# Loads to both halves of the partitions split in two, and the transposed solutions of both batches in one bank

## The chip, the cores and the metric

The kernel runs on one core of one Trainium2 chip. The metric is the device time of one execution, in microseconds (us). Before the change it was 1447.63 us, the median of three runs (1440.06 to 1449.23).

## The reference

Three stages are chained. The first is a recurrence over 768 time steps on a 40 by 40 state, for 4 batches and 8 heads; the other two are two-layer networks over the 3072 tokens that it yields (320 to 2048 to 320), the first with x·relu6(x+3)/6 between its layers, the second with x·sigmoid(x).

```python
B, H, S, D = 4, 8, 768, 40
for t in range(S):
    kt, vt, rt = (k[:, :, t], v[:, :, t], r[:, :, t])
    wt, at, bt = (w[:, :, t], a[:, :, t], b[:, :, t])
    y[:, :, t] = np.einsum('bhd,bhde->bhe', rt, state)
    Sa = np.einsum('bhde,bhe->bhd', state, at)
    state_decay = state * wt[:, :, None, :] - np.einsum('bhd,bhe->bhde', Sa, bt)
    state = state_decay + np.einsum('bhd,bhe->bhde', vt, kt)
...
h = x @ w_in
g = h * np.clip(h + 3.0, 0.0, 6.0) / 6.0
x = g @ w_out
...
h = x @ w_in
g = h * (1.0 / (1.0 + np.exp(-h)))
return g @ w_out
```

## The kernel before, in words

**The recurrence** is worked in chunks of 32 time steps. A pair of batches is taken at a time; a window is 128 time steps of a pair (12 windows in all), and a chunk, called a step below, is a quarter of a window (48 steps). The steps form a chain, because each starts from the state that the step before left. For each window three things are prepared: products of the decays (`prepare`), the 32 by 32 triangular matrices of all chunks and heads (`windows`, L452), and the inverses of these matrices. For the inverses the matrices go to DRAM (`scr_l`, L476), come back into the tile u with one matrix to a partition (`factors`, L489), are inverted on VectorE in 30 rounds of two operations (`inverses`, L515 and L519), and go back by way of `scr_t` (L535, L540). There are 64 matrices in a window, and each is laid on two partitions, 64 apart, since VectorE inverts one half of the rows on each. So one load of `factors` reads 64 rows of 4 KB twice: its source is broadcast with a leading dimension of two. The tile u has two places; one of them lies in the stage buffer of the weights.

One step of the chain (`steps`), for both batches: L613 makes the right-hand sides, which ScalarE copies to rx; L626 transposes the state; L642 makes the transposed solution and L644 the plain one, batch by batch, into one bank of PSUM for each batch; VectorE copies the transposed solution out (L650, `turned`), ScalarE the plain one (L655, `evac`); L667 needs the transposed solutions of both batches; VectorE masks its result (L675); L692 makes the outputs and the new state from it and from the plain solutions; and the new state is copied out for the next step. The chain has three banks of PSUM.

**The two networks** run in tiles of 256 tokens, 12 tiles for each. In a tile the first product (`first`, L937) has 128 matmuls and the second (`second`, L981) 96. A tile of the first network needs the outputs of one window; the second network starts when the first has ended. The weights come as 64-bit floats, in 16 chunks for each network, and are turned into pairs of 32-bit values by a sequence on VectorE, ScalarE and GpSimd (`convert`, `split`; L780 to L805). A chunk is loaded by three DMAs: L742 and L752 with full width, and L745, which brings rows 256 to 319 of the first matrix to both halves of the partitions, with a source that is broadcast in the same way as that of L489. The first 64 of the last 128 rows are so held twice, for two products at once. The same is done for the last 64 of the 320 channels of the decays (L879) and outputs (L884) in `inputs1`. The weights of the second network lie where the recurrence had its tiles, and are loaded when it has ended.

**The order of the work** is written out before the program is built: the class `Order` keeps a time for each engine, generators ask for an engine with a duration and conditions, and the earliest candidate is taken, by priority. Each engine, and SP, which issues all the DMAs, then works its list in order. The durations of these lists are the planner's; in an engine's list, whatever stands behind an instruction that waits, waits too.

Of the kernel before, what the change touches and what calls it, by code (L numbers as in the profile page):

```python
# [16 lines left out]
B, H, S, D = 4, 8, 768, 40  # L17
BH = B * H
NB = 2
NP = B // NB  # L20
G = NB * H
HP = H // 2
NW, WT, CT = 6, 128, 32
NC = WT // CT
# [7 lines left out]
DM, DFF = H * D, 2048  # L32
NM = DFF // 128
MT = NB * WT
SEG = WT + 1
NWX = 5 * SEG
E0 = 64
# [208 lines left out]
class Kernel:  # L246
# [232 lines left out]
    def factors(self):  # L479

        nc, o = self.nc, self.o
        for n in range(NN):
            k = n % 2 if n > 1 else 0
            u = self.u[k]
            free = [("uo", n - 1) if n < 3 else ("iv", n - 2)] if n else []
            if k:
                free += self.converted
            el = yield ("sp", 524e3, ("lo", n), *free)
            nc.sync.dma_start(out=u.rearrange("p j i -> p (j i)"),  # L489
                              in_=self.scr_l[n % 2].unsqueeze(0).to_broadcast([2, G * NC, CT * CT]))  # L490
            o.ev[("u", n)] = o.t["sp"]
            o.ev[("ul", n)] = el

# [75 lines left out]
    def steps(self, bs, chunks):  # L569

        nc, o = self.nc, self.o
        rxs = [self.rx[32:64, b] for b in range(NB)]
# [9 lines left out]
        def every(conds):  # L582

            return [(b, tuple(c for x in bs for c in conds(x)) if b == bs[0] else ()) for b in bs]
# [4 lines left out]
        for g in chunks:  # L589
            n, c = divmod(g, NC)  # L590
            ga, ysl = self.ga[n % 3], self.ysl[g % 2]
# [7 lines left out]
            if first:  # L599
                for b in bs:  # L600
                    e = yield ("pool", 500.0, *st[b])
# [6 lines left out]
            for b, conds in every(lambda x: (("ga", n), ("v", g), *st[x])):  # L608
                e = yield ("pe", 600.0, "bank", *conds)
                p = o.take()  # L610
                pv = p[:, 0:DM].rearrange("p (h e) -> p h e", h=H)
                for h in range(H):
                    nc.tensor.matmul(out=pv[32:64, h], lhsT=ga[0:KP, b * H + h, c * CT:(c + 1) * CT],  # L613
                                     rhs=self.rhs[0:KP, b, h], start=True, stop=True)
                o.ev[("x0", g, b)] = e

                def evac(p=p, pv=pv, b=b):
                    nc.scalar.activation(out=rxs[b][:, :, 0:D], in_=pv[32:64], func=AF.Copy)
                    o.give(p, o.t["act"] + 190)
                o.one("act", 440.0, [e], evac, ("rx", g, b))  # L620
            for b, conds in [] if first else every(lambda x: st[x]):
                e = yield ("pe", 300.0, "bank", *conds)
                p = o.take()
                pv = p[0:D, 0:DM].rearrange("p (h e) -> p h e", h=H)
# [6 lines left out]
                o.one("act", 440.0, [e], evac, ("st", g, b))  # L631


            for b, conds in every(lambda x: [("rx", g, x)]):
                e = yield ("pe", 1050.0, "bank", *conds)
                p = o.take()
                pv = p[:, 0:DM].rearrange("p (h e) -> p h e", h=H)
                pt = p[:, DM:DM + HP * CT].rearrange("p (h t) -> p h t", h=HP)
                gs = [ga[32:64, b * H + h, c * CT:(c + 1) * CT] for h in range(H)]
                for h in range(H):  # L640
                    r0 = E0 * (h % 2)
                    nc.tensor.matmul(out=pt[r0:r0 + 64, h // 2], lhsT=rxs[b][:, h], rhs=gs[h], start=True, stop=True)  # L642
                for h in range(H):
                    nc.tensor.matmul(out=pv[32:64, h], lhsT=gs[h], rhs=rxs[b][:, h, 0:D], start=True, stop=True)  # L644
                if c == NC - 1:
                    o.ev[("gafree", n, b)] = e
                done = o.share(p, 2)

                def turned(pt=pt, b=b, done=done):
                    nc.vector.tensor_copy(out=self.vr[:, b, 3], in_=pt)  # L650
                    done(o.t["dve"] + 160)
                o.one("dve", 290.0, [e], turned, ("xt", g, b))

                def evac(pv=pv, b=b, done=done):
                    nc.scalar.activation(out=self.ysr[32:64, b, :, CT:RW], in_=pv[32:64], func=AF.Copy, scale=-1.0)  # L655
                    done(o.t["act"] + 190)
                o.one("act", 440.0, [e], evac, ("xv", g, b))


            e = yield ("pe", 40.0 + 215.0 * len(bs), "bank", *[("xt", g, b) for b in bs], ("vr", g, 0), ("vr", g, 1))  # L660
            p = o.take()
            pv = p[:, 0:H * CT].rearrange("p (h t) -> p h t", h=H)
            for h in range(HP):
                for x in range(2):
                    for b in bs:
                        r0 = 64 * b + 32 * x
                        nc.tensor.matmul(out=pv[r0:r0 + 32, 2 * h:2 * h + 2], lhsT=self.vr[0:KP, b, 1 + 2 * x, h],  # L667
                                         rhs=self.vr[0:KP, b, 0::2, h], start=True, stop=True)
            done = o.share(p, len(bs))
# [13 lines left out]
            for b, conds in every(lambda x: (  # L683
# [3 lines left out]
                e = yield ("pe", 600.0, "bank", *conds)  # L687
                p = o.take()
                pv = p[:, 0:4 * RW].rearrange("p (h n) -> p h n", h=4)
                for h in range(4):  # L690
                    for u in range(2):
                        nc.tensor.matmul(out=pv[E0 * u:E0 * u + D, h], lhsT=ysl[0:KP, b, 4 * u + h],  # L692
                                         rhs=self.ysr[0:KP, b, 4 * u + h], start=True, stop=True)
                o.ev[("yse", g, b)] = e
                done = o.share(p, 2)
# [33 lines left out]
    def raws(self, wi, wo, key):  # L729

        nc, cv = self.nc, self.cv
        for m in range(NM):
            if wi.dtype == mybir.dt.float32:
                k, wiv, wov = 1, wi, wo
            else:
                k, wiv, wov = 2, wi.bitcast(I32), wo.bitcast(I32)
            cs = slice(m * 128 * k, (m + 1) * 128 * k)
            raw, free = self.slot("raw0", key, m)
            raw = raw.bitcast(wiv.dtype)
            yield ("sp", 131e3 * k, free and ("cv", key, free[0], 0), ("u", 0) if key == 1 and m >= GR else None,  # L740
                   ("uo", NN - 1) if key == 2 else None)
            nc.sync.dma_start(out=raw[:, 0:256 * k].rearrange("p (j f) -> p j f", j=2),  # L742
                              in_=wiv[0:256, cs].rearrange("(j p) f -> p j f", p=128))
            e = yield ("sp", 66e3 * k)
            nc.sync.dma_start(  # L745
                out=raw[:, 256 * k:384 * k],
                in_=wiv[256:320, cs].unsqueeze(0).to_broadcast([2, 64, 128 * k]))
            self.o.ev[("raw", key, m, 0)] = e
            raw, free = self.slot("raw1", key, m)
            raw = raw.bitcast(wiv.dtype)  # L750
            e = yield ("sp", 164e3 * k, free and ("cv", key, free[0], 1))
            nc.sync.dma_start(out=raw[:, 0:DM * k], in_=wov[m * 128:(m + 1) * 128])  # L752
            self.o.ev[("raw", key, m, 1)] = e
# [111 lines left out]
    def inputs1(self):  # L865

        nc, o = self.nc, self.o
        xs = self.xw[0].rearrange("p (j b t) -> p j b t", j=3, b=NB)
        ws = self.xw[1].rearrange("p (j b t) -> p j b t", j=3, b=NB)
        xf, wf = (x.rearrange("p (j n) -> p j n", j=3) for x in self.xw)  # L870
        for n in range(NN):
            free = ("xp", n - 1) if n else ("cv", 1, K0 - 1, 1)
            sw, sy = self.scr_w[n], self.scr_y[n]
            for b in range(NB):
                r = sw[b * DM:(b + 1) * DM, 0:WT]
                yield ("sp", 131e3, ("wo", n), free, ("cv", 1, K0 - 1, 0))
                nc.sync.dma_start(out=ws[:, 0:2, b], in_=r[0:256].rearrange("(j p) t -> p j t", p=128))
                yield ("sp", 66e3)
                nc.sync.dma_start(out=ws[:, 2, b], in_=r[256:DM].unsqueeze(0).to_broadcast([2, 64, WT]))  # L879
            g = n * NC + NC - 1  # L880
            e1 = yield ("sp", 262e3, *[("yo", g - q, b) for b in range(NB) for q in (0, 2)])
            nc.sync.dma_start(out=xf[:, 0:2], in_=sy[0:256].rearrange("(j p) b t -> p j (b t)", p=128))
            e = yield ("sp", 131e3)
            nc.sync.dma_start(out=xf[:, 2],  # L884
                              in_=sy[256:DM].rearrange("p b t -> p (b t)").unsqueeze(0).to_broadcast([2, 64, MT]))
            xh, xl = self.xh[n % 2], self.xl[n % 2]
            e = yield ("pool", 1840.0, e, e1)
            nc.gpsimd.tensor_tensor(out=xf, in0=xf, in1=wf, op=ALU.mult)
            e = yield ("act", 850.0, e, ("g1", n - 2) if n > 1 else None)
            nc.scalar.activation(out=xh, in_=xf, func=AF.Copy)  # L890
            yield ("pool", 1310.0, e)
            nc.gpsimd.tensor_tensor(out=xl, in0=xf[:, 0:2], in1=xh[:, 0:2].bitcast(F32), op=ALU.subtract)
            e = yield ("pool", 790.0)
            nc.gpsimd.tensor_tensor(out=xh[64:128, 2], in0=xf[64:128, 2], in1=xh[64:128, 2].bitcast(F32),
                                    op=ALU.subtract)
            o.ev[("xp", n)] = o.ev[("x", n)] = e
# [316 lines left out]
```

## Time and profile before

| | |
|---|---|
| median of three runs | 1447.63 us |
| profiled execution, its own time | 1440.64 us |
| span of its trace | 1438.8 us |
| TensorE (PE) busy | 1230.8 us, 86% of the span |
| VectorE (DVE) busy | 792.4 us, 55% |
| ScalarE (ACT) busy | 571.9 us, 40% |
| GpSimd (POOL) busy | 427.8 us, 30% |
| DMA: moved, mean rate | 149.47 MB, 104 GB/s |
| mean granted clock of TensorE | 0.892 |

The profile is of one execution. A busy share is an average over very different stages: in the first stage the weights of the first network are converted and the first windows are prepared; then the recurrence and the first network share TensorE; then the recurrence has ended, the first network is finished and the weights of the second are loaded; at last the second network runs alone. A granted clock of 1.00 is 2.4 GHz and 0.50 is 1.2 GHz, the two levels that TensorE has; a value between them is a mean over time. SPq is the queue of DMA issues: a row of SPq tells how long an issue took, not how long the transfer did; a DMA row of the chain of waits runs from the issue to the landing.

### The profile page before, as it was taken

Reading aid. Unit: us, or ns where it says so; the run is one execution under the profiler, and the core shown is the slowest. Engines: PE = TensorE matmul, PEld = TensorE weight load, DVE = VectorE, ACT = ScalarE, POOL = GpSimd, SP = SyncE. Lnnn points to the kernel's source line nnn. Section 1 sums busy time; section 2 is a strip of 40 time slices with the busy share of each in tenths; the row PEclk is TensorE's granted clock in tenths of the full one; section 3 lists DMA queues with packets and bytes.
Section 4 is the critical chain, followed back from the end, with each engine's and each line's share of the span. In section 5 each row is a group of like instructions: output and inputs, shape, how many; then the busy total and the mean of one; then the engine's idle time right before and its main releaser. Section 6 shows DMA issues by size and latency. Waiting matters only on the chain.

```text
span 1438.8 us, 35403 instructions
## 1 busy us (share of the span) xinstructions
PE 1230.8 (86%) x14582; PEld 1146.6 (80%) x14582; DVE 792.4 (55%) x1852; ACT 571.9 (40%) x1177; POOL 427.8 (30%) x532
## 2 busy tenths in 40 slices
PE   1035658899989998899989999877899999999998
PEld 1034557788878888788878888777799999999998
DVE  6486668585588576686866522377762222222221
ACT  3232334444334333434433344455644333343333
POOL 6334344334352342423432232376420000000000
PEclk9999857888898777877977898998999999999999
DMA  6573756437657556665663221344511000010000
GB/s 214 146 169 109 178 160 150 108 75 190 155 143 186 128 145 148 162 187 142 156 167 86 53 69 41 83 99 105 119 39 43 21 21 21 21 41 21 21 10 22
DMA packets 245419, 149.47 MB, mean 104 GB/s; under 512 B 144256, under 2 KB 230400, under 8 KB 245248
## 3 DMA queue, kind: packets, MB, share of 16 engines
q1 hardware_dynamic: 245248, 147.12, 40.2%
q8 instruction: 117, 1.92, 0.6%
q14 instruction: 54, 0.44, 0.1%
HBM read 104.58 MB, written 42.50 MB: 102 GB/s over the span
## 4 chain that ended last, share of the span: by engine, by line
PE 57%; DMA 20%; DVE 14%; issue 3%; ACT 3%; SPq 2%; POOL 1%; ACTq 0%; DVEq 0%; POOLq 0%
PE ph L937 20%; PE po L981 20%; DMA u<-scr_l 6%; DMA stage<-in_w2i 4%; DVE uh L519 4%; DVE ut L515 4%; PE r L644 4%; PE r L642 3%; PE r L613 3%; DMA stage<-in_w1i 3%; PE r L692 2%; PE r L667 2%; DMA scr_t<-uh 2%; PE r L626 2%; DMA scr_l<-ga 1%
## 5 line engine op out<-in xcount | busy, mean ns | idle before, releaser
L937 PE MATMUL ph<-xh,w 128*128 128x256 f32 x2304 | 399.1, 303 | 27.5 <-DVE t L952 27.5
L981 PE MATMUL po<-w,gh 128*128 128x320 f32 x1536 | 404.1, 330 | 2.6 <-ACT xo L997 2.6
L937 PEld LDWEIGHTS ph<-xh,w 128*128 128x128 f32 x2304 | 340.2, 206 | 39.0 <-DVE t L952 31.3
L981 PEld LDWEIGHTS po<-w,gh 128*128 128x128 f32 x1536 | 285.0, 201 | 11.3 <-issue 3.9
L981 PE MATMUL po<-w,gl 128*128 128x320 f32 x768 | 249.8, 325 | 12.5 <-POOL gl L960 7.8
L963 DVE TENSOR_TENSOR gl<-t,gh 128x512 fp32r<-128x512 f32 x118 | 84.5, 717 | 247.1 <-ACT gh L957 246.8
L937 PE MATMUL ph<-xl,w 128*128 128x256 f32 x768 | 168.1, 303 | 0.0
L981 PEld LDWEIGHTS po<-w,gl 128*128 128x128 f32 x768 | 155.1, 202 | 15.2 <-POOL gl L960 9.5
L957 ACT ACTIVATE gh<-t 128x512 fp32r<-128x512 f32 x192 | 120.9, 630 | 75.9 <-DVE t L952 65.8
L960 POOL TENSOR_TENSOR gl<-t,gh 128x512 fp32r<-128x512 f32 x74 | 95.7, 1295 | 127.2 <-ACT gh L957 106.4
L954 ACT ACTIVATE t<-ph 128x512 f32<-128x512 f32 x96 | 57.3, 597 | 191.6 <-PE ph L937 191.5
L937 PEld LDWEIGHTS ph<-xl,w 128*128 128x128 f32 x768 | 131.2, 207 | 2.5 <-issue 0.3
L519 DVE TENSOR_TENSOR uh<-uh,ut 128x30 f32<-128x30 f32 (+4 forms) x360 | 122.3, 340 | 10.4
L613 PE MATMUL r<-rhs,ga 104*32 104x40 f32 x1536 | 74.8, 216 | 37.2 <-DVE rhs L708 20.4
L613 PEld LDWEIGHTS r<-rhs,ga 104*32 104x32 f32 x1536 | 68.2, 124 | 45.5 <-DVE rhs L708 22.1
L560 POOL COPY ysr<-rhs 32x640 f32<-32x640 f32 x48 | 34.3, 715 | 216.0 <-PE r L692 196.1
L515 DVE TENSOR_TENSOR ut<-uh,u 128x30 f32<-128x30 f32 (+7 forms) x210 | 71.4, 340 | 46.3 <-ACT uh L509 40.6
L950 ACT ACTIVATE t<-ph,con 128x512 f32<-128x512 f32 x96 | 65.3, 684 | 79.2 <-PE ph L937 63.7
L644 PE MATMUL r<-rx,ga 32*32 32x40 f32 x1536 | 88.4, 219 | 0.1
L655 ACT ACTIVATE ysr<-r 32x320 f32<-32x320 f32 x96 | 41.0, 428 | 103.1 <-DVE vr L650 77.4
L644 PEld LDWEIGHTS r<-rx,ga 32*32 32x32 f32 x1536 | 75.3, 125 | 4.8 <-issue 0.2
L692 PE MATMUL r<-ysr,ysl 104*40 104x72 f32 x1536 | 64.8, 243 | 13.3 <-DVE ysr L675 4.8
(122 smaller groups left out, 1603.9 us busy)
## 6 DMA issues: line engine op xcount, KB each, us to landing
ld<-in_pre SPq DMA_DIRECT2D x12, 960.0 KB
vr<-in_vr SPq DMA_DIRECT2D x96, 80.0 KB
scr_n<-kbn SPq DMA_DIRECT2D x12, 640.0 KB
ysl<-scr_n SPq DMA_DIRECT2D x48, 160.0 KB
s<-scr_kb SPq DMA_DIRECT2D x46, 160.0 KB
ld<-scr_kb SPq DMA_DIRECT2D x40, 160.0 KB
stage<-in_w2o SPq DMA_DIRECT2D x16, 320.0 KB
scr_kb<-ld SPq DMA_DIRECT2D x12, 384.0 KB
```

What stands on the lines that cost most here:

```text
L515: nc.vector.tensor_tensor(out=tv, in0=uh[:, 0:r, j:j + 1].to_broadcast([128, r, m]), in1=u[:, j:j + 1, j + 1:CT].to_broadcast([128, r, m]) ...
L519: nc.vector.tensor_tensor(out=uh[:, 0:r, j + 1:CT], in0=uh[:, 0:r, j + 1:CT], in1=tv, op=ALU.add)
L613: nc.tensor.matmul(out=pv[32:64, h], lhsT=ga[0:KP, b * H + h, c * CT:(c + 1) * CT], rhs=self.rhs[0:KP, b, h], start=True, stop=True)
L644: nc.tensor.matmul(out=pv[32:64, h], lhsT=gs[h], rhs=rxs[b][:, h, 0:D], start=True, stop=True)
L692: nc.tensor.matmul(out=pv[E0 * u:E0 * u + D, h], lhsT=ysl[0:KP, b, 4 * u + h], rhs=self.ysr[0:KP, b, 4 * u + h], start=True, stop=True)
L937: nc.tensor.matmul(out=p[:, h * MT:(h + 1) * MT], lhsT=seq[q][0], rhs=seq[q][1], start=q == 0, stop=q == 7)
L950: nc.scalar.activation(out=t, in_=p, func=AF.Relu, bias=self.three)
L954: nc.scalar.activation(out=t, in_=p, func=AF.Silu)
L957: nc.scalar.activation(out=gh, in_=t, func=AF.Copy)
L960: nc.gpsimd.tensor_tensor(out=gl, in0=t, in1=gh.bitcast(F32), op=ALU.subtract)
L963: nc.vector.tensor_tensor(out=gl, in0=t, in1=gh.bitcast(F32), op=ALU.subtract)
L981: nc.tensor.matmul(out=self.po[s], lhsT=l, rhs=r, start=m == 0 and q == 0, stop=m == NM - 1 and q == 2)
```

## The change

Five loads that brought the same rows to both halves of the partitions in one DMA, with a broadcast source, are now two DMAs each, one to partitions 0 to 63 and one to 64 to 127, with a plain source. In a step, L642's work for both batches goes into one bank, ahead of L644's for either; one copy of VectorE takes both out; each plain solution has a bank for itself. The durations that the planner is told follow.

```diff
@@ factors
-            el = yield ("sp", 524e3, ("lo", n), *free)
-            nc.sync.dma_start(out=u.rearrange("p j i -> p (j i)"),
-                              in_=self.scr_l[n % 2].unsqueeze(0).to_broadcast([2, G * NC, CT * CT]))
+            for x in range(2):
+                el = yield ("sp", 262e3, ("lo", n), *free)
+                nc.sync.dma_start(out=u[64 * x:64 * x + 64].rearrange("p j i -> p (j i)"), in_=self.scr_l[n % 2])
@@ steps
-            for b, conds in every(lambda x: [("rx", g, x)]):
-                e = yield ("pe", 1050.0, "bank", *conds)
+            e = yield ("pe", 400.0 * len(bs), "bank", *[("rx", g, b) for b in bs])
+            p = o.take()
+            pt = p[:, 0:NB * HP * CT].rearrange("p (b h t) -> p b h t", b=NB, h=HP)
+            gs = {(b, h): ga[32:64, b * H + h, c * CT:(c + 1) * CT] for b in bs for h in range(H)}
+            for b, h in gs:
+                r0 = E0 * (h % 2)
+                nc.tensor.matmul(out=pt[r0:r0 + 64, b, h // 2], lhsT=rxs[b][:, h], rhs=gs[b, h], start=True, stop=True)
+
+            def turned(p=p, pt=pt):
+                nc.vector.tensor_copy(out=self.vr[:, bs[0]:bs[-1] + 1, 3], in_=pt[:, bs[0]:bs[-1] + 1])
+                o.give(p, o.t["dve"] + 160)
+            o.one("dve", 430.0, [e], turned, ("xt", g, bs[0]))
+            for b in bs:
+                e = yield ("pe", 620.0, "bank")
                 p = o.take()
                 pv = p[:, 0:DM].rearrange("p (h e) -> p h e", h=H)
...
-                    nc.tensor.matmul(out=pt[r0:r0 + 64, h // 2], lhsT=rxs[b][:, h], rhs=gs[h], start=True, stop=True)
-                for h in range(H):
-                    nc.tensor.matmul(out=pv[32:64, h], lhsT=gs[h], rhs=rxs[b][:, h, 0:D], start=True, stop=True)
+                    nc.tensor.matmul(out=pv[32:64, h], lhsT=gs[b, h], rhs=rxs[b][:, h, 0:D], start=True, stop=True)
...
-                def turned(pt=pt, b=b, done=done):
-                    nc.vector.tensor_copy(out=self.vr[:, b, 3], in_=pt)
-                    done(o.t["dve"] + 160)
-                o.one("dve", 290.0, [e], turned, ("xt", g, b))
@@ raws
-            e = yield ("sp", 66e3 * k)
-            nc.sync.dma_start(
-                out=raw[:, 256 * k:384 * k],
-                in_=wiv[256:320, cs].unsqueeze(0).to_broadcast([2, 64, 128 * k]))
+            for x in range(2):
+                e = yield ("sp", 33e3 * k)
+                nc.sync.dma_start(out=raw[64 * x:64 * x + 64, 256 * k:384 * k], in_=wiv[256:320, cs])
@@ inputs1
-                yield ("sp", 66e3)
-                nc.sync.dma_start(out=ws[:, 2, b], in_=r[256:DM].unsqueeze(0).to_broadcast([2, 64, WT]))
+                for x in range(2):
+                    yield ("sp", 33e3)
+                    nc.sync.dma_start(out=ws[64 * x:64 * x + 64, 2, b], in_=r[256:DM])
...
-            e = yield ("sp", 131e3)
-            nc.sync.dma_start(out=xf[:, 2],
-                              in_=sy[256:DM].rearrange("p b t -> p (b t)").unsqueeze(0).to_broadcast([2, 64, MT]))
+            for x in range(2):
+                e = yield ("sp", 66e3)
+                nc.sync.dma_start(out=xf[64 * x:64 * x + 64, 2], in_=sy[256:DM].rearrange("p b t -> p (b t)"))
```

The planner's durations differ, so the whole order is another one. Two places of it follow; line numbers of the changed kernel are one higher from L650 on (L489 is now L490, L642 is L640, L644 is L651).

SP's queue where the factors of the third window are loaded (u<-scr_l; in_w1i and in_w1o are the weights of the first network, in_pre and scr_w, scr_a, scr_kb belong to the preparation of windows, vr and rhs to the steps). Before:

```order
L742 DMA stage<-in_w1i 128x2x256
L745 DMA stage<-in_w1i 128x1x256
L752 DMA stage<-in_w1o 128x640
L472 DMA ga_137<-scr_a 40x16x128
L535 DMA scr_t<-uh 1024x1x32 x2
L476 DMA scr_l<-ga_137 32x64x32
L546 DMA rhs<-in_vt 32x640
L540 DMA ga_136<-scr_t 32x64x32
L315 DMA ga_135<-in_pre 128x645
L316 DMA ld<-in_pre 128x1920
L489 DMA u<-scr_l 128x1x1024
```

With the change:

```order
L752 DMA stage<-in_w1o 128x640
L472 DMA ga_137<-scr_a 40x16x128
L880 DMA xw_105<-scr_w 64x128 x2
L546 DMA rhs<-in_vt 32x640
L476 DMA scr_l<-ga_137 32x64x32
L344 DMA scr_a<-ld 128x5x128
L349 DMA wct_145<-scr_w 40x16x1
L551 DMA vr<-in_vr 40x2x256 x2
L369 DMA scr_kb<-ld 128x3x256
L565 DMA ysl_131<-scr_n 64x640
L369 DMA scr_kb<-ld 128x2x256
L490 DMA u<-scr_l 64x1024 x2
```

What moved: the load of the third window's factors was the 110th row of SP's list and stood before four chunks of weights; now it is the 151st, and stands behind the last chunk.

PE's list at the last step of the recurrence (L613, L626, the solutions, L667 and L692 as above; L937 here is work of the first network; r_154 to r_156 are the three banks). Before:

```order
L626 MATMUL r_155<-con,rhs 40x40 x8
L937 MATMUL ph_121<-xl_109,w_13_101 128x256 x2
L642 MATMUL r_154<-ga_137,rx 64x32 x8
L644 MATMUL r_154<-rx,ga_137 32x40 x8
L642 MATMUL r_156<-ga_137,rx 64x32 x8
L644 MATMUL r_156<-rx,ga_137 32x40 x8
L937 MATMUL ph_121<-xh_107,w_13_101 128x256 x4
L937 MATMUL ph_119<-xh_107,w_14_102 128x256 x2
L937 MATMUL ph_119<-xl_109,w_14_102 128x256 x2
L667 MATMUL r_155<-vr 32x64 x16
```

With the change:

```order
L626 MATMUL r_155<-con,rhs 40x40 x8
L640 MATMUL r_156<-ga_137,rx 64x32 x16
L651 MATMUL r_154<-rx,ga_137 32x40 x8
L651 MATMUL r_155<-rx,ga_137 32x40 x8
L668 MATMUL r_156<-vr 32x64 x16
L938 MATMUL ph_120<-xh_107,w_4_92 128x256 x4
```

What moved: the plain solutions stand between the transposed ones and the products that need them, where matmuls of the network stood. Counted over PE's whole list, 1024 matmuls of L937 and 744 of L981 stand ahead of the end of the last step before, 944 and 696 with the change.

## Rows read from the trace of the kernel before

**Rows 1.** Busy time by stage: from, to, length, each engine (instructions), granted clock, DMA share, GB/s

```profile
0.00:230.00 230.00, 94.22 (x1326) 82.36 (x1326) 155.97 (x380) 75.25 (x166) 102.84 (x135) 0.89 0.61 160
230.00:436.40 206.40, 191.05 (x2575) 174.13 (x2576) 139.40 (x349) 82.34 (x173) 84.84 (x107) 0.84 0.55 140
436.40:913.80 477.40, 458.12 (x7075) 408.30 (x7075) 298.23 (x835) 185.83 (x420) 149.36 (x207) 0.82 0.50 124
913.80:1077.60 163.80, 132.37 (x918) 127.32 (x917) 109.53 (x161) 90.88 (x186) 90.73 (x84) 0.95 0.40 96
1077.60:1438.80 361.20, 355.09 (x2696) 354.44 (x2694) 89.26 (x130) 137.59 (x233) 0.00 (x0) 1.00 0.08 24
```

**Rows 2.** Chain of waits, the broadcast loads on it: start, us, what

```profile
45.33 14.60 DMA u<-scr_l
...
88.56 7.40 DMA stage<-in_w1i
...
107.16 16.39 DMA u<-scr_l
...
152.21 7.36 DMA stage<-in_w1i
161.75 7.72 DMA stage<-in_w1i
181.49 16.43 DMA stage<-in_w1i
...
263.62 14.27 DMA stage<-scr_l
...
370.73 14.67 DMA u<-scr_l
...
592.44 13.32 DMA u<-scr_l
```

**Rows 3.** Chain of waits, two loads without a broadcast

```profile
1.20 3.36 DMA ga<-in_pre
...
144.69 4.51 DMA ld<-scr_kb
```

**Rows 4.** Timeline of SP's queue: start, us that the issue took, line

```profile
50.11 10.32 SPq L752 DMA_DIRECT2D xw<-in_w1o  x1
...
60.96 0.53 SPq L745 DMA_DIRECT2D xw<-in_w1i  x1
...
593.71 11.79 SPq L546 DMA_DIRECT2D rhs<-in_vt  x1
```

**Rows 5.** Busy time while two of the u loads run (columns as in the first group)

```profile
48.00:59.00 11.00, 0.00 (x0) 0.00 (x0) 0.00 (x0) 0.00 (x0) 0.00 (x0) 1.00 0.54 154
594.50:604.50 10.00, 10.00 (x144) 9.10 (x146) 2.40 (x6) 1.97 (x4) 6.32 (x12) 0.66 0.27 71
```

**Rows 6.** Chain of waits where the second network's weights are loaded

```profile
915.90 6.42 DMA stage<-in_w2i
...
1026.69 5.52 DMA stage<-in_w2i
```

**Rows 7.** Waits: who waited for whom, us in total, times, longest

```profile
ACT ysr L655 <- DVE vr L650: 77.4, 57, 7.0
...
PE ph L937 <- DVE t L952: 27.5, 16, 3.9
...
DVE stage L786 <- DMA stage<-in_w2i: 21.3, 9, 6.4
...
PE r L667 <- DVE vr L650: 13.4, 9, 3.7
```

**Rows 8.** Chain of waits: matmuls of the networks at full clock, and one solution's copy

```profile
215.17 0.30 DVE vr L650
...
1128.03 3.84 PE ph L937 x32
1131.87 3.52 PE po L981 x24
```

More of the change, by code (lines that the diff above doesn't have):

```diff
@@ L636, in steps @@
+            def turned(p=p, pt=pt):
[4 more added lines that the diff above has]
+                e = yield ("pe", 620.0, "bank")
                 p = o.take()
                 pv = p[:, 0:DM].rearrange("p (h e) -> p h e", h=H)
-                pt = p[:, DM:DM + HP * CT].rearrange("p (h t) -> p h t", h=HP)
@@ L639, in steps @@
-                gs = [ga[32:64, b * H + h, c * CT:(c + 1) * CT] for h in range(H)]
                 for h in range(H):
-                    r0 = E0 * (h % 2)
-                    nc.tensor.matmul(out=pt[r0:r0 + 64, h // 2], lhsT=rxs[b][:, h], rhs=gs[h], start=True, stop=True)
-                for h in range(H):
-                    nc.tensor.matmul(out=pv[32:64, h], lhsT=gs[h], rhs=rxs[b][:, h, 0:D], start=True, stop=True)
+                    nc.tensor.matmul(out=pv[32:64, h], lhsT=gs[b, h], rhs=rxs[b][:, h, 0:D], start=True, stop=True)
@@ L645, in steps, with evac @@
                 if c == NC - 1:
                     o.ev[("gafree", n, b)] = e
-                done = o.share(p, 2)
-                def turned(pt=pt, b=b, done=done):
-                    nc.vector.tensor_copy(out=self.vr[:, b, 3], in_=pt)
-                    done(o.t["dve"] + 160)
-                o.one("dve", 290.0, [e], turned, ("xt", g, b))
-                def evac(pv=pv, b=b, done=done):
+                def evac(p=p, pv=pv, b=b):
                     nc.scalar.activation(out=self.ysr[32:64, b, :, CT:RW], in_=pv[32:64], func=AF.Copy, scale=-1.0)
-                    done(o.t["act"] + 190)
+                    o.give(p, o.t["act"] + 190)
@@ L657, in steps @@
                 o.one("act", 440.0, [e], evac, ("xv", g, b))
-            e = yield ("pe", 40.0 + 215.0 * len(bs), "bank", *[("xt", g, b) for b in bs], ("vr", g, 0), ("vr", g, 1))
+            e = yield ("pe", 40.0 + 215.0 * len(bs), "bank", ("xt", g, bs[0]), ("vr", g, 0), ("vr", g, 1))
             p = o.take()
```

## The prediction, made before the changed kernel ran

> **What bounds the kernel now.** I read the table by stage first, then the chain of waits inside each stage, then SP's queue and the waits of the engines that the change touches.
>
> The table by stage [rows 1] shows five stretches. In the first 230 us TensorE is busy for 94.2 us; it waits. From 230 to 436.4 (where the first step of the fifth window starts) it is busy for 191 of 206 us, and from there to the end of the last step, at 913.8, for 458 of 477, at a granted clock of 0.82. Then 163.8 us in which the first network is finished while the second one's weights arrive, 132 of them busy. The last 361.2 us are the second network alone, busy throughout at full clock: the change has nothing there.
>
> So three things can give time back: waiting at the start, some 19 us of idle TensorE in the long stretch, and what the fourth stretch takes above its work.
>
> The chain of waits says what the start waits for. Of the first 436 us, eight rows are loads to both halves of the partitions [rows 2]: four of the factors (14.60, 16.39, 14.27, 14.67: 59.9 us) and four of the first network's weights (7.40, 7.36, 7.72, 16.43: 38.9 us), 98.8 us together. They are slow for their size. The factors move 512 KB in 14.60 us, 36 GB/s; the load at the start of the program, to all 128 partitions, moves 322.5 KB in 3.36 us, 98 GB/s [rows 3]. While the first factors are loaded (48 to 59 us) no engine is busy at all [rows 5]. And the loads hold more than their readers: the issue right behind them took 10.32 and 11.79 us, where an issue takes about 0.53 [rows 4]. SP's queue stands as long as the load runs, and in that time DMA moves 71 GB/s with 27% of its engines [rows 5]. I read this as a transfer confined to few of the 16 DMA engines, with what comes later queued behind it there.
>
> **The loads.** Twelve loads of factors, 32 of weights, 24 of decays and 12 of outputs become two each: 80 issues more, at 0.53 us [rows 4] 42 us of SP's time over the program. I put nothing of this on the path, because single issues of 10 to 12 us go away; if they do not, the 42 us are a cost (third rival).
>
> What does a pair take? The trace has no such load. Below, 3.36 us [rows 3] and one issue more, 3.9; above, what the broadcast takes, 14.6. Between them lies the last of four loads to 32 partitions each, 4.51 us [rows 3]. I take 4.5 for the factors, as nearest in form (several DMAs to parts of the partitions behind one another), and 3.5 for the smaller weights. Then the eight rows cost 4 × 4.5 + 4 × 3.5 = 32 instead of 98.8 us: 67 us less on the chain.
>
> The Trainium skill has a rule against this: "DMA: Bandwidth & Descriptors", section "Rules for kernel authors", says of two transfers to disjoint partition halves not to bother, as they serialize on the same 16 engines, and to use one 128-partition transfer. By it the 67 us would be none. The same table says that an outermost broadcast dimension of c copies confines a DMA to at most c engines, and by that the 67 us stand. The 36 against 98 GB/s and the 27% speak for the second sentence in this kernel.
>
> Not all of the 67 come off the start. VectorE is busy for 156 of the first 230 us and for 139 of the next 206 [rows 1]: converting the weights, preparing windows and inverting lie between the loads, and a load that lands earlier often meets VectorE with other work. I take two thirds, 45 us, for 0 to 436.4.
>
> **The long stretch (436.4 to 913.8).** Three of its six loads of factors are on the chain (13.32 is one of them [rows 2]), but TensorE is busy for 96% here, so what they free is at most the idle 19 us. Of the idle time 13.4 us are L667 waiting for the copy of the transposed solution [rows 7] (over the whole run). With the change the plain solutions, 16 matmuls, stand between the last transposed solution and L668, and cover one copy for both batches; the old copy took 0.30 us [rows 8]. The copy of a plain solution no longer waits for VectorE's copy of the same bank, which cost ScalarE 77.4 us [rows 7], beside other work. In the place of the wait removed, the second batch's plain solution now needs a third bank, and waits for ScalarE's copy of a transposed state. I take 10 us back here for loads and steps together; the bounds are -5 (the new wait for a bank costs more than the old one) and 19.
>
> The new order also moves work of the network. Counted in PE's lists from the start of the fifth window to the end of the last step, there are 552 matmuls of L937 and 420 of L981 instead of 592 and 462. At 3.84/32 = 0.120 us and 3.52/24 = 0.147 us [rows 8] that is 40 × 0.120 + 42 × 0.147 = 11 us at full clock, 13 at 0.82. The stretch gives -23 us in all.
>
> **The fourth stretch.** Before, 512 matmuls of L937 and 408 of L981 are left at the end of the last step: 61.4 + 59.8 = 121.2 us at full clock, in 163.8: 42.6 us are lost. The chain there is the weights' loads, ten rows between 916 and 1033 us, the first of 6.42 and the last of 5.52 us [rows 6]; VectorE waits 21.3 us for them, and TensorE 27.5 us for VectorE's half of the first network's nonlinearity [rows 7], which stands behind those conversions in VectorE's list. With the change 592 and 456 matmuls are left: 71.0 + 66.9 = 137.9 us. There is more to hide the weights under, and each chunk's wait falls from about 5.5 to about 3.5 us. I leave 15 us lost: 153 instead of 163.8, -11. Bounds: nothing gained (137.9 + 42.6 = 180.5, +17) and nearly all (143, -21).
>
> **The sum.** -45 - 23 - 11 = -79 us on a span of 1438.8: 1360, and 1362 as the profiled execution counts its own time (1440.64). The median of the runs, 1447.63, is 0.5% above the profiled one; I put 1364.
>
> **The rivals.**
>
> 1. *VectorE is next* (0.22). The loads get short, but converting and inverting set the pace: only 20 of the 67 us come off the start, 5 instead of 10 off the long stretch, and the fourth one loses 30 instead of 15 (168, +4). For it: VectorE's 68% in the first two stretches. Against: the 11 us without any work in [rows 5]. -20 - 18 + 4 = -34: 1407.
> 2. *The queue was the bound* (0.10). With SP no longer held, nearly all of the 67 us come off, the 19 idle us too, and a denser TensorE is granted 0.86 instead of 0.82 in the long stretch (477 × (1 - 0.82/0.86) = 22 us). -67 - 13 - 41 - 21 = -142: 1299. Against: a busy share of 96% already, at that clock.
> 3. *The halves serialize* (0.06): a pair takes as long as the broadcast, 14.6 us, with 0.53 us of issue added. Then the loads give nothing, the steps 10 us, the moved matmuls cancel (-13, +17): -6, 1435. The skill's first rule is this rival. For it: both transfers are issued by one queue. Against: the 98 GB/s of a load from the same queue.
> 4. *The block ahead of the third window* (0.04), the slower side. Counted in PE's lists, 120 matmuls of L938 and 108 of L982 now stand between steps 8 and 9, 18 and 33 before: 30.2 instead of 7.0 us at full clock, because the third window's factors moved behind the last chunk of weights in SP's queue. That is 23 us, 28 at the clock of 0.84 [rows 1]. If the chain of steps is then what ends last and the loads free less than 28 us ahead of it, the start is longer: with nothing freed 1440.6 + 28 = 1469. Against: in the old trace the chain stood for long between steps 16 and 17 anyway, waiting for the fifth window, and what is late at step 9 is absorbed there.
>
> **How the numbers follow.** The forecast has 0.58. Its own bounds: with a third of the 67 us and nothing in the fourth stretch 1395, with the better end of each term 1315. The range is 1297 to 1418: it takes in the forecast, most of rival 1 and about half of rival 2, 0.8 in all. About 1% is what a measurement of this kernel can tell from no change. Faster by over 1%: forecast and rivals 1 and 2, 0.90. Within 1%: rival 3, 0.06. Slower: 0.04.
>
> **What would show it.** The chain of waits has rows of u of 4 to 5 us and of weights of 3 to 4; SP has no issue of 10 us behind them. The first step of the fifth window starts near 390 us and the last step ends near 845. ScalarE no longer waits for VectorE at the plain solution (L656), TensorE hardly at L668. The fourth stretch has a chain of matmuls instead of weights. I am wrong if the rows of u stay above 10 us (rival 3), if they shorten and the chain fills with VectorE's lines at the same starts (rival 1), or if step 9 starts later than before (rival 4).

## The result: 1348.9 us, 0.932 of the time before

The changed kernel took 1348.9 us (median of four runs, 1344.1 to 1355.38); the kernel before, on the same chip, 1448.43. The ratio is 0.932, with a 95% interval of 0.926 to 0.938. The forecast was 1364 in a range of 1297 to 1418. The profiled execution took 1344.1 us; its span is 1342.3.

The table by stage of the changed kernel answers to [rows 1], with the same borders: the first step of the fifth window, the end of the last step, the last 361.2 us. The columns are from, to, length, busy time of TensorE, its weight loads, VectorE, ScalarE and GpSimd (instructions), the granted clock, the DMA share and GB/s.

```profile
0.00:230.00 230.00, 131.06 (x1868) 118.59 (x1868) 182.64 (x414) 96.27 (x208) 122.33 (x158) 0.84 0.70 186
230.00:388.40 158.40, 139.14 (x2018) 125.91 (x2018) 123.15 (x317) 61.43 (x131) 63.15 (x82) 0.86 0.69 158
388.40:819.50 431.10, 416.11 (x6962) 376.10 (x6961) 293.81 (x783) 179.41 (x411) 145.36 (x204) 0.85 0.55 132
819.50:981.10 161.60, 145.78 (x1050) 141.00 (x1049) 130.89 (x167) 94.78 (x195) 101.51 (x88) 0.98 0.32 98
981.10:1342.30 361.20, 354.55 (x2692) 353.90 (x2690) 88.74 (x130) 137.43 (x232) 0.00 (x0) 1.00 0.08 24
```

The fifth window's first step starts 48 us earlier, at 388.4. The long stretch takes 431.1 instead of 477.4. The fourth takes 161.6 instead of 163.8, with 132 matmuls more in it. The last is what it was.

The loads of [rows 2] have all but left the chain of waits. By engine the chain of before had 20% DMA; now it has this (the page's fourth part, first line):

```profile
PE 64%; DVE 20%; issue 5%; DMA 4%; POOL 3%; SPq 2%; ACT 2%; DVEq 0%; POOLq 0%; ACTq 0%
```

Of the five loads one pair is left among the 195 longest pieces of the chain, at 340.51 (the decays, L880). The row of weights at 20.56 is a chunk's full-width load (L743), and the longest DMA row is the write of the matrices that precedes the factors:

```profile
20.56 4.39 DMA stage<-in_w1i
...
34.07 8.84 DMA scr_l<-ga
...
340.51 1.93 DMA xw<-scr_w
```

How long a pair takes is seen in the timeline, where the first factors are loaded: the issues, and then the readers of either half, each with the idle time ahead of it and what ended that in brackets.

```profile
42.92 1.08 SPq L490 DMA_DIRECT2D u<-scr_l  x2
...
46.25 0.63 ACT L509 ACTIVATE uh<-u 64x512 f32<-64x512 f32 x1 [1.71 <-DMA u<-scr_l]
...
47.31 0.42 DVE L506 COPY uh<-u 64x512 f32<-64x512 f32 x1 [3.27 <-DMA u<-scr_l]
```

The second half is read 47.31 - 42.92 = 4.4 us after the first issue; the broadcast took 14.60. The single packets that the two traces record say why. Each load of factors is 128 packets of 4 KB. Before, in each of the twelve windows, they went two at a time and took 10.3 to 12.8 us from the first to the last; with the change they go 8 to 14 at a time on average and the 128 take 2.3 to 3.6 us. And what stands behind the pair is issued at once, where [rows 4] had an issue of 11.79 us for the same load of rhs:

```profile
581.03 1.24 SPq L490 DMA_DIRECT2D stage<-scr_l  x2
582.37 0.52 SPq L546 DMA_DIRECT2D rhs<-in_vt  x1
582.99 0.37 SPq L315 DMA_DIRECT2D stage<-in_pre  x1
```

The waits that answer to [rows 7] (who waited for whom: us in total, times, longest):

```profile
ACT ysr L656 <- PE r L651: 71.2, 64, 2.9
...
PE ph L938 <- DVE t L953: 22.3, 13, 5.9
...
PE r L668 <- DVE vr L643: 12.2, 6, 3.0
...
DVE stage L786 <- DMA stage<-in_w2i: 1.0, 1, 1.0
```

ScalarE does not wait for VectorE at the plain solutions any more, but it waits nearly as long (71.2 us) for TensorE there; TensorE waits for the copy of the transposed solutions nearly as before; VectorE's wait for the weights is gone.

### The profile page after: what moved, and what is told of

Read it like the earlier page. It is cut to its first block, busy times and chain, and to the rows that moved or that the text cites. A ratio compares the mean times of both kernels' runs of the same rounds, so it can differ in the third digit from the quotient of the medians.

```text
span 1342.3 us, 35538 instructions
## 1 busy us (share of the span) xinstructions
PE 1186.6 (88%) x14582; PEld 1115.5 (83%) x14582; DVE 819.2 (61%) x1805; ACT 569.3 (42%) x1177; POOL 432.4 (32%) x532
## 4 chain that ended last, share of the span: by engine, by line
PE 64%; DVE 20%; issue 5%; DMA 4%; POOL 3%; SPq 2%; ACT 2%; DVEq 0%; POOLq 0%; ACTq 0%
PE po L982 22%; PE ph L938 22%; DVE ut L515 4%; DVE uh L519 4%; PE r L651 4%; PE r L693 3%; PE r L613 3%; PE r L640 3%; PE r L668 2%; PE r L626 2%; PE r L452 1%; DVE t L953 1%; DVE stage L801 1%; DVE ld L336 1%; DVE stage L789 1%
## 5 line engine op out<-in xcount | busy, mean ns | idle before, releaser
L982 PE MATMUL po<-w,gh 128*128 128x320 f32 x1536 | 399.7, 329 | 4.0 <-ACT gh L958 4.0
L938 PE MATMUL ph<-xh,w 128*128 128x256 f32 x2304 | 380.1, 294 | 22.7 <-DVE t L953 22.3
L938 PEld LDWEIGHTS ph<-xh,w 128*128 128x128 f32 x2304 | 324.9, 198 | 33.0 <-DVE t L953 26.0
L964 DVE TENSOR_TENSOR gl<-t,gh 128x512 fp32r<-128x512 f32 x118 | 87.7, 746 | 247.0 <-ACT gh L958 246.6
L938 PE MATMUL ph<-xl,w 128*128 128x256 f32 x768 | 160.1, 291 | 0.3 <-POOL xl L893 0.3
L961 POOL TENSOR_TENSOR gl<-t,gh 128x512 fp32r<-128x512 f32 x74 | 97.3, 1320 | 170.0 <-ACT gh L958 148.3
L519 DVE TENSOR_TENSOR uh<-uh,ut 128x30 f32<-128x30 f32 (+4 forms) x360 | 123.0, 342 | 10.7
L938 PEld LDWEIGHTS ph<-xl,w 128*128 128x128 f32 x768 | 124.4, 197 | 1.9 <-POOL xl L893 0.5
L693 PE MATMUL r<-ysr,ysl 104*40 104x72 f32 x1536 | 70.7, 256 | 13.5 <-DVE ysr L676 12.4
L651 PE MATMUL r<-rx,ga 32*32 32x40 f32 x1536 | 82.0, 221 | 0.0
L613 PE MATMUL r<-rhs,ga 104*32 104x40 f32 x1536 | 73.6, 215 | 8.1 <-DMA ga<-scr_t 3.6
L613 PEld LDWEIGHTS r<-rhs,ga 104*32 104x32 f32 x1536 | 67.2, 123 | 16.2 <-DVE rhs L709 4.6
L693 PEld LDWEIGHTS r<-ysr,ysl 104*40 104x40 f32 x1536 | 62.2, 138 | 22.3 <-issue 10.6
L515 DVE TENSOR_TENSOR ut<-uh,u 128x30 f32<-128x30 f32 (+7 forms) x210 | 75.7, 360 | 8.0 <-ACT uh L509 2.0
L651 PEld LDWEIGHTS r<-rx,ga 32*32 32x32 f32 x1536 | 74.3, 127 | 3.4 <-ACT ysr L656 0.4
```

Source lines behind the costliest of these rows:

```text
L515: nc.vector.tensor_tensor(out=tv, in0=uh[:, 0:r, j:j + 1].to_broadcast([128, r, m]), in1=u[:, j:j + 1, j + 1:CT].to_broadcast([128, r, m]) ...
L519: nc.vector.tensor_tensor(out=uh[:, 0:r, j + 1:CT], in0=uh[:, 0:r, j + 1:CT], in1=tv, op=ALU.add)
L651: nc.tensor.matmul(out=pv[32:64, h], lhsT=gs[b, h], rhs=rxs[b][:, h, 0:D], start=True, stop=True)
L938: nc.tensor.matmul(out=p[:, h * MT:(h + 1) * MT], lhsT=seq[q][0], rhs=seq[q][1], start=q == 0, stop=q == 7)
L961: nc.gpsimd.tensor_tensor(out=gl, in0=t, in1=gh.bitcast(F32), op=ALU.subtract)
L964: nc.vector.tensor_tensor(out=gl, in0=t, in1=gh.bitcast(F32), op=ALU.subtract)
```

## The experiments

Every ratio is to the kernel before, run on the same chip. Times of stages are from one profiled execution each. Four kernels (the change and the three of the section on the fourth stretch) have the same lists up to the last step; in them the fifth window starts at 388.4 to 397.2 us and the long stretch takes 431.1 to 444.4, so a stage is known to some 10 us. Line numbers are those of each kernel.

| | median, us | ratio (95%) | fifth window starts | last step ends | span |
|---|---|---|---|---|---|
| before | 1448.43 | 1 | 436.4 | 913.8 | 1438.8 |
| the change | 1348.9 | 0.932 (0.926 to 0.938) | 388.4 | 819.5 | 1342.3 |
| loads split, lists of before | 1350.77 | 0.929 (0.925 to 0.933) | 386.2 | 830.8 | 1341.8 |
| broadcasts, lists of the change | 1453.71 | 0.999 (0.996 to 1.002) | 452.5 | 933.0 | 1462.1 |
| factors alone split | 1370.8 | 0.943 (0.938 to 0.947) | 394.9 | 843.0 | 1366.3 |
| weights alone split | 1431.64 | 0.984 (0.980 to 0.989) | 423.8 | 904.6 | 1418.2 |
| loads split, steps as before, new lists | 1347.49 | 0.928 (0.923 to 0.933) | 373.5 | 827.1 | 1338.5 |
| split, and 512 KB more on few engines, SP | 1424.01 | 0.979 (0.975 to 0.984) | 422.6 | 903.1 | 1414.6 |
| the same issued by ScalarE | 1453.52 | 1.000 (0.996 to 1.004) | 435.2 | 945.1 | 1456.2 |
| split, and 512 KB more, spread | 1354.18 | 0.932 (0.926 to 0.939) | 391.4 | 841.4 | 1352.4 |

### The loads without the new lists, and the new lists without the loads

The first kernel is that before, with the five loads split inside the same entry of the planner, so that every engine's list stays the same:

```diff
             el = yield ("sp", 524e3, ("lo", n), *free)
-            nc.sync.dma_start(out=u.rearrange("p j i -> p (j i)"),
-                              in_=self.scr_l[n % 2].unsqueeze(0).to_broadcast([2, G * NC, CT * CT]))
+            for x in range(2):
+                nc.sync.dma_start(out=u[64 * x:64 * x + 64].rearrange("p j i -> p (j i)"), in_=self.scr_l[n % 2])
```

> The kernel before with all five loads split in two, while the planner is told nothing: every engine's list stays that of before, but for the second DMA of each pair. Theory A (the gain is the short loads and the queue that they free): 1350 to 1370 us, ratio 0.935 to 0.946, within 20 us of the change's 1348.9; rows of u at 4 to 5 us, no issue of 10 us. Theory B (the new steps and the new order of the lists give a part of their own, 30 us or more of the 100): 1385 us or more, 0.956 or more.

The second is the changed kernel with one broadcast DMA issued after each pair of the planner's entries.

> The changed kernel with its five loads put back to one broadcast DMA each, under the changed kernel's lists. Theory A: the gain is lost, 1430 to 1460 us, ratio 0.988 to 1.01. Theory B: 1410 us or less, 0.975 or less, since the steps' new form stays. A third reading, that the changed lists are laid out for short loads and stall on long ones: above 1460.

1350.77 and 1453.71: theory A holds on both sides. The loads alone give all of the gain; the new steps and the new lists without them give nothing that can be measured (0.999, 0.996 to 1.002).

The stretches of the first of the two, whose lists are those of before, show what short loads do to the same work:

```profile
386.20:830.80 444.60, 438.56 (x7076) 389.88 (x7075) 301.15 (x841) 185.27 (x420) 150.83 (x209) 0.86 0.57 134
830.80:980.60 149.80, 130.15 (x920) 125.04 (x919) 119.93 (x162) 88.87 (x186) 94.36 (x84) 0.97 0.37 106
```

Against the third and fourth of [rows 1] the long stretch is 33 us shorter for the same matmuls. 13 of that is idle time (19.3 to 6.0); 20 is busy time, 438.6 instead of 458.1, at a clock of 0.86 instead of 0.82 (busy time times clock is nearly the same, 376 and 377). The fourth is 14 us shorter.

### Which of the loads

> The kernel before with the load of the factors alone split, lists as before. Twelve loads fall from some 14.6 to some 4.5 us. If the time is lost where the chain of waits passes through them (four of them before the fifth window, two to three after it): 4 x 10 us at the start, of which two thirds come off, and 10 to 20 us later: 1390 to 1410 us. If most of the gain comes from the queue behind them: nearer 1370. If the start is paced by the weights: 1420 or more.

> The kernel before with the broadcast part of the weights' chunks alone split (32 loads), lists as before. By my sums some 15 of the 25 us on the chain at the start, and 10 to 25 us in the stretch where the second network's weights are loaded: 1400 to 1425 us. If the weights are paced by their conversion on VectorE and GpSimd, not by the loads: 1430 or more.

The factors alone give 1370.8, 81% of what the five loads give in the same comparison (1455.8 - 1370.8 = 85 of 1455.8 - 1350.8 = 105 us); the weights alone 1431.64, 24 us. The two add up (109). I had expected less of the factors, by their place on the chain, and the lower figure was the one named for the queue behind them. The weights came 7 us short of what was expected, in the range named for conversion. The fourth stretch, from the last step's end to 361.2 us before the span's end, is 162.0 us with the factors alone split and 152.3 with the weights alone: what it gave back belongs to the weights.

### The steps

The changed kernel with the steps as before, laid out anew by the planner:

> The five loads split and told to the planner as in the change; the steps stay as before. What the steps' new form is worth among short loads, in an order that the planner lays out for each. My prediction's term of 10 us: 1355 to 1365. Nothing, as the last pair of runs suggests: 1340 to 1355.

1347.49, the ratio 0.928 beside the change's 0.932. The new form of the steps is worth nothing that can be measured here. TensorE's wait for the copy is 12.2 us with it, where this kernel has the first and the kernel of the old lists with split loads the second of these rows:

```profile
PE r L667 <- DVE vr L650: 20.6, 13, 5.4
...
PE r L667 <- DVE vr L650: 19.6, 16, 5.0
```

But 7 to 8 us of waiting for the copy do not show in the time.

### Why a broadcast is slow

In the changed kernel the matrices are written to DRAM twice, and loaded by one DMA without a broadcast: for even windows from two places with a gap between them, for odd ones from one place of 128 rows.

```diff
             for x in range(2):
                 el = yield ("sp", 262e3, ("lo", n), *free)
-                nc.sync.dma_start(out=u[64 * x:64 * x + 64].rearrange("p j i -> p (j i)"), in_=self.scr_l[n % 2])
+            nc.sync.dma_start(out=u.rearrange("p j i -> p (j i)"), in_=self.scr_l[n % 2][:, 0:G * NC])
...
-            self.scr_l = dr.tile([2, G * NC, CT * CT], F32, name="scr_l")
+            self.scr_l = [dr.tile([2, G * NC + 1 - k, CT * CT], F32, name=f"scr_l{k}") for k in range(2)]
```

> The changed kernel, but the factors' matrices are written to DRAM twice and the load is one DMA again, without a broadcast. For even windows the two copies lie with a gap of a row between them, so that the source keeps a leading dimension of two; for odd ones they lie end to end, so that it has one of 128. If the leading dimension sets how many DMA engines work: even windows' rows near 12 to 15 us from issue to landing, odd ones' 4 to 5. If the repeated reading of the same rows was what was slow: 4 to 5 us for both. Time: between 1350 and 1410 us by the first, near 1350 by the second.

The chain of waits of this kernel; the window numbers are 0, 1, 2, 4, 8 and 10, in order of time:

```profile
44.30 15.65 DMA u<-scr_l
...
106.81 5.05 DMA u<-scr_l
...
208.47 14.37 DMA u<-scr_l
...
344.09 14.58 DMA u<-scr_l
...
547.64 13.70 DMA u<-scr_l
...
668.50 13.53 DMA u<-scr_l
```

The even windows take 13.5 to 15.7 us though no row is read twice; the one odd window on the chain takes 5.05. The packets show it for all twelve windows: in the six even ones the 128 packets go two at a time and take 11.4 to 13.8 us, in the six odd ones 7 to 13 at a time, in 2.1 to 3.6. So it is the leading dimension of two, not the broadcast. This kernel's one run took 1396.54 us: half of the loads long, about half of the gain lost.

### What the long load costs: its readers, the queue behind it, or its engines

To the first kernel of these experiments (split loads, lists of before) a DMA is added behind each pair, which nobody reads:

```diff
+            nc.sync.dma_start(out=self.scr_d[:, :, 0:CT * CT], in_=self.scr_l[n % 2].unsqueeze(0).to_broadcast([2, G * NC, CT * CT]))
```

> All five loads split under the old lists (1350.8 us), and behind each pair of loads of the factors a DMA from DRAM to DRAM that nobody waits for, with the old load's shape: 512 KB, a broadcast source with a leading dimension of two, rows of 4 KB. The readers of u have their data as early as with short loads, while what stands behind in SP's queue is held as it was before. If the gain came from what stood behind the loads: 1400 to 1430 us. If from the readers of u: 1350 to 1375.

1424.01: 73 us of the 105 are lost again, though the readers of u have their data as early as without the extra DMA: ScalarE and VectorE stand 8.6 us for u, and 9.0 without it. What others stand for is longer:

```profile
POOL ysr L559 <- DMA vr<-in_vr: 48.5, 15, 11.1
POOL ysr L561 <- DMA rhs<-in_vt: 38.8, 6, 9.1
...
ACT uh L510 <- DMA scr_t<-uh: 22.8, 3, 10.0
...
DVE uh L507 <- DMA u<-scr_l: 5.1, 1, 5.1
...
ACT uh L510 <- DMA u<-scr_l: 3.5, 1, 3.5
```

The same transfers can be compared one by one with the kernel without the extra DMA, since the lists are the same. Of those that SP issues within 12 us behind the extra DMA, 18 have a wait that tells of their landing in both traces: they land 13.9 us after their issue (median), for 4.8 without it. All others stay at 3.6. Ten of SP's issues take 4 to 12 us (75 us in all; one of 5.0 us without it), and five more wait for the extra DMA to land (24 us).

So I took the order of SP's queue for the cause, and tried the same DMA from ScalarE's queue, with rows of an input as its source, so that ScalarE waits for nothing:

```diff
+            nc.scalar.dma_start(out=self.scr_d[:, :, 0:CT * CT],
+                                in_=self.i["pre"][n, 0:64, 0:CT * CT].unsqueeze(0).to_broadcast([2, G * NC, CT * CT]))
```

> All five loads split under the old lists (1350.8 us), and beside each pair of loads of the factors a DMA of the old load's shape (512 KB to DRAM, a broadcast source with a leading dimension of two, rows of 4 KB) that nobody waits for, issued by ScalarE's queue instead of SP's. The same few DMA engines are as long at work as with the extra transfer on SP's queue (1424 us), but nothing of SP's stands behind it in one queue. If the queue is what held the work: 1350 to 1375 us. If the sharing of those engines: 1400 to 1430.

1453.52, the whole gain lost and more than from SP's queue. That reads as the end of the theory of the queue's order, but this kernel does not take SP's queue out of the way. SP's own waits have these rows, and the chain of waits has the DMA with 8% of the span:

```profile
SPq L490 <- DMA scr_d<-in_pre: 66.8, 5, 15.4
SPq L553 <- DMA scr_d<-in_pre: 14.6, 1, 14.6
SPq L748 <- DMA scr_d<-in_pre: 14.2, 1, 14.2
```

With five rows of 11.0 to 13.1 us these are twelve waits, 155 us in all, one for each extra DMA. Each time the issue that waits is the next one with the same completion semaphore (the counter that tells of a DMA's landing), and SP's list stands behind it until the extra DMA has landed. So somebody does wait for it, and the readers of u wait as well, because five of the twelve waits are of the issue of u itself:

```profile
POOL ysr L560 <- DMA vr<-in_vr: 73.9, 21, 13.4
...
POOL ysr L562 <- DMA rhs<-in_vt: 53.9, 7, 11.5
...
ACT uh L511 <- DMA u<-scr_l: 44.0, 11, 14.0
```

What ScalarE's queue does show is smaller. Nine transfers that SP issued from its own queue within 12 us behind such a DMA landed 8.2 us after their issue (median), where the same nine took 4.2 without it.

The control has the same bytes from the factors' source, at the same place in SP's queue, in two plain DMAs:

> The control to the extra transfer on SP's queue (1424 us): the same 512 KB from the same source to the same place in DRAM, at the same place in SP's queue, but as two plain DMAs of 64 rows. If few engines for a long time were the cost: 1350 to 1365 us. If any extra 512 KB behind each load costs that much: 1400 or more.

1354.18, 3 us more than without them, within the intervals (0.932 and 0.929). The extra 6 MB cost nothing that can be measured; that a leading dimension of two carries them costs 73 us on SP's queue. Of the 27 transfers behind these DMAs that can be compared, the median is 4.9 us for 4.7.

So a long load costs mostly what stands behind it, not its readers. On its own queue the transfers behind it land some 9 us later, and from another queue some 4 us later. How much of the 103 us on ScalarE's queue is that, and how much is SP's standing for the landing, was not separated; a kernel in which no issue of SP shares a semaphore with the extra DMA would tell. That the transfers beside it are late because each has a part on the few DMA engines that the long one holds fits the packets that go two at a time, but no view lists the engines one by one, so it is not shown directly.

The sums of the engines' waits for a DMA go with the times, added over the rows of the waits' view (SP's own are not in it): 363 us before, 97 with the change; 79 with the split loads under the old lists, 280 with the extra DMA behind them, 364 with it on ScalarE's queue, 119 with the control.

### The fourth stretch

It lost 161.6 - 137.9 = 24 us in the changed kernel, where I had said 15. The chain there has 76 us of GpSimd and VectorE, conversions and low halves above all, and 47 us of TensorE, where the prediction's sign was a chain of matmuls. Three kernels asked which of them paces it. The first deals the low halves of five tiles to both engines in turn:

```diff
-        if layer == 1 and i < GD:
+        if layer == 1 and (i < GA or i < NN and k % 2 == 0):
```

with GA = 7.

> The changed kernel; in the last five tiles of the first network the low halves of the second product's operands are taken by GpSimd and VectorE in turn, instead of GpSimd in the tiles up to the ninth and VectorE in the last three. If the fourth stretch (161.6 us for 137.9 us of matmuls) is paced by whichever of the two has both these and the conversions: 1335 to 1345 us. If by the loads of the weights still: 1349, no change. If the planner's new order costs elsewhere: above 1355.

The others shorten one operation of the conversion on either engine, and so leave out the low bits of the second network's weights on GpSimd, or their sign and top bit on VectorE:

> The changed kernel under its own lists; for the second network's weights GpSimd's addition in the conversion (L791, 32 of them, 33.4 us of GpSimd in the fourth stretch) works on 32 columns instead of 384 or 320: the weights' low bits are left out. If GpSimd paces the fourth stretch (161.6 us for 137.9 us of matmuls): 1332 to 1342 us. If the loads or VectorE do: 1345 to 1352.

> The same with VectorE: its second operation of the conversion (L789, 32 of them, 36 us of VectorE in the fourth stretch) works on 32 columns; the weights' sign and top bit are left out for the rest. If VectorE paces the fourth stretch: 1328 to 1342 us. If the loads or GpSimd do: 1345 to 1352.

1346.34, 1337.56 and 1345.15 us; ratios 0.927 (0.921 to 0.933), 0.922 (0.914 to 0.930) and 0.924 (0.919 to 0.930). None is apart from the change's 0.932 (0.926 to 0.938) by more than the intervals. The stretch itself is steadier than the whole (149.8, 150.4, 149.9 and 149.8 us in the four kernels with the same lists and split loads): it takes 157.9, 147.4 and 154.1 us, for 161.6, with the same matmuls in it. TensorE's idle time in it says more: 15.8 us with the change, 15.7, 6.7 and 10.7 in the three. Dealing out the low halves gave no idle time back; shortening GpSimd's operation gave 9 us, VectorE's 5. So GpSimd's conversions pace most of what is idle there, by one profile each; that the time of the whole falls with it is not shown.

## Why the prediction was right, point by point

**The loads.** The step rested on the rate of 36 against 98 GB/s, and on taking 4.5 us for a pair. A pair took 4.4 where it can be read, and its packets 2.3 to 3.6 in all twelve windows. What was inferred, a transfer that goes by few engines and holds up others far beyond its readers, held: two packets at a time, and 73 us lost with the readers served early. Of the two sentences of the Trainium skill ("DMA: Bandwidth & Descriptors", "Rules for kernel authors") the one on a small outermost dimension agrees with the even and odd windows above (two packets at a time and 11.4 to 13.8 us against 2.1 to 3.6). By the one against two transfers to disjoint halves the pair would have given nothing; here, where the one transfer has a leading dimension of two, the measurement goes against it (4.4 us for 14.60).

**The start**: -45 forecast, -48 measured. The two thirds that I took off the 67 us were a choice, so that it came out this close is luck: in the three other kernels with the same lists up to there the start is 39 to 47 us earlier. VectorE's share of it rose as rival 1 has it, from 68% to 79% of the first 230 us, but did not set a pace that kept the loads from paying.

**The long stretch**: -23 forecast, -46 measured. This is the term that was mis-sized. I had bounded the gain by the 19 us of idle TensorE. Of the 46 us only 4 are idle time (19.3 to 15.0) and 42 are busy time: the 82 matmuls of the network that moved, as forecast (13 us), 32 of L452 that moved too and that the count left out (8 us at 248 ns, their mean there before), and for the most part of the rest a granted clock of 0.85 instead of 0.82. With unchanged lists the loads took 13 us of idle time and 20 us of busy time, at 0.86 (13 and 16 with the factors alone split, 14 and 13 in the control). What rival 2 said of the clock is true in that, though nothing else of that rival is. The share of busy time was no bound: with the shorter loads the clock rose too. Under the old lists it was 0.86, 0.86 and 0.85 with the factors split (all loads, factors alone, the control), and 0.82, 0.83, 0.83 and 0.79 with a long load left in (before, weights alone, the two extra DMAs). Under the new lists it was 0.85, 0.83, 0.84 and 0.82 in four kernels with the same work there, so of the 46 us some 13 are within the spread of single executions. Why the clock rises was not tried. The 10 us that I put down for loads and steps together are covered by the loads alone; the steps' part is none within some 6 us. Its mechanism failed in one point: TensorE still waits for the copy of the transposed solutions (12.2 us for 13.4). In each of the six waits VectorE was at the rounds of the inversion (L515, L519) when the solutions were there, and the copy stood behind them in its list.

**The fourth stretch**: -11 forecast, -2 measured. The weights' loads stopped mattering, as said (VectorE's wait for them fell from 21.3 to 1.0 us), but behind them stood the conversions, GpSimd's first: rival 1's mechanism in another place. 24 us were lost instead of 15.

**The rivals.** Rival 3, the halves serialize: the loads took 4.4 us; out. Rival 4: the block of matmuls between steps 8 and 9 is there (207.3 to 266.7 us from the end of one to the end of the other), but step 9 ended 8 us earlier than before, at 266.7 for 275.1; it was absorbed, as the case against it had it. The sum, -96 us on the span for -79, lies between the forecast and rival 2. One figure of the prediction is a slip: its better ends (-67, -32 and -21 from 1440.6) add up to some 1320, not 1315; nothing rests on it.

## What to carry to other kernels

A DMA whose outermost dimension is two was slow for its size here, and most of its cost was borne by what stood behind it, its readers being the smaller share; look for one wherever a transfer's rate is a fraction of another's, and give it a leading dimension that is long (128 here). An engine that is busy 96% of a stretch can still gain more than its idle time if its granted clock is below full, as this one did. A wait that is removed from a chain's lists is worth nothing until the time of the whole says so: put the old order under the new loads, and the new order under the old loads, before crediting either. And before a DMA that nobody reads is taken for one that nobody waits for, look at the waits of the queue that issues the others.

## What was not expected of the hardware

A transfer of 512 KB two packets at a time, which no engine reads, costs 73 us in all when twelve of them stand in SP's queue behind the loads (1424.01 for 1350.77); the same bytes in plain DMAs cost nothing that can be measured (1354.18). A queue of its own did not make it cheaper (1453.52): transfers beside it still landed in 8.2 us for 4.2, and SP stood 155 us for its landing. SP's issues of 10 to 12 us are one sign of such a transfer, but not the only one: in the kernel with ScalarE's queue no issue takes over 5 us, and the standing shows in SP's waits instead.
